# Key norms of the second and third round taken from the diagonals of the keys' products

## The chip, the cores and the metric

One core of one Trainium2 chip runs the whole program. The metric is the device time of one execution in microseconds; lower is better. TensorE is called PE here, VectorE DVE, ScalarE ACT, GpSimd POOL and SyncE, whose queue issues nearly all transfers, SP.

## What is computed

Three stages follow each other. The first is a delta-rule attention over two batches of eight heads, 768 tokens of 48 numbers each; the second an MLP with a rational activation; the third a layer of eight experts with one expert for each token. Cut to what matters:

```
# attention, for each (batch, head):
k_n = k / (np.linalg.norm(k, axis=-1, keepdims=True) + 1e-06)
for t in range(S):
    y[:, :, t] = np.einsum('bhd,bhde->bhe', q[:, :, t], state)
    v_old = np.einsum('bhde,bhd->bhe', state, kt)
    state = state + bt[:, :, :, None] * np.einsum('bhd,bhe->bhde', kt, vt - v_old)
# MLP: 1536 tokens, 384 -> 2048 -> 384
h = x @ w_in
P = a[0] + a[1] * h + a[2] * h2 + a[3] * h3
Q = 1.0 + np.abs(b[0]) * np.abs(h) + np.abs(b[1]) * h2
x = (P / (Q + 1e-06)) @ w_out
# experts: argmax and softmax of x @ w_gate; expert 384 -> 1024 -> 384
h = np.maximum(np.einsum('ecd,edf->ecf', disp, w1), 0.0)
y = np.einsum('ecf,efd->ecd', h, w2)
```

The norm of each key enters twice: in gamma, which is beta divided by the square of (norm + 1e-6), and as nrm, norm + 1e-6, by which the values are multiplied so that the keys need not be divided.

## The kernel before

The 768 tokens are 12 chunks of 64, in three rounds of four chunks. The 16 pairs of batch and head lie in two halves of the partitions, eight pairs in each.

For each round r the following is done. `load_kk(r)` (L138) brings the round's keys to SBUF, with tokens on partitions, in two transfers (L142); they lie in a buffer of the tag "raw", of which there are two, shared with the raw MLP weights that `conv` turns from 64-bit to 32-bit numbers (L188 load, L194 to L207) and later with the raw expert weights (L743). `norm(r)` (L212) squares them on ACT (L216), sums the squares on DVE into ss (L217, two instructions for 32 columns), and works out on 128x32 numbers the root (L222 on DVE, Ln and Exp on ACT, L223 and L224), nrm and gamma (L225 to L231), and gamma's transpose gamT (L233). `gram(n)` (L236) multiplies the keys of chunk n with themselves on PE, and ACT copies 32x32 blocks into Wu. `solve(r)` (L254) inverts the triangular systems of all pairs of the round at once on DVE: a memset of its result buffer on POOL (L258), a transpose in blocks of 32x32 from Wu to bufT (L259), the product with gamma (L262), 31 pairs of a product and a sum (L269, L272), and two transposes at the end (L275, L276).

For each chunk n: `values(n)` (L322) multiplies the values by nrm on POOL (L327, two instructions). `lower(n)` (L280, its products L302 and L304) completes the inverse on PE; `tk` (L335) and `qk` (L345) are products with the keys; U (L365), S (L377) and Y (L389) are the new values, the state and the result, each copied by ACT or DVE; L404 to L412 turn Y to the layout in which the MLP takes it.

The MLP works in 48 tiles of 128x512 numbers, in six blocks of 256 tokens. Each tile has a product h on PE (L460), nine element-wise instructions shared by ACT (L465, L466, L476, L477, and L487 for gh), DVE (L469, L470, L478, L479, L480) and POOL (L467, L468, and L488 for gl), and a product with the second weights on PE (L502, or L520 for the last block). gh and gl are the upper and lower part of the activation. After each block follows the gate of its tokens (L540 to L598). Expert weights come in by L743, are split by ACT (L744) and DVE (L745). The first rows of experts 0 to 2 are computed early, between the last tiles: hidden layer (L808, L812, L813), result y (L825), its weighting yo (L829) and a scatter of rows to the output on POOL (L831). L753 gathers rows for an expert.

What sets the order: each step is entered with `add(name, time, needs, f)`, where the time comes from a table of numbers, PLAN. The steps are emitted by time, those that they need first. A scheduler with a simulated timeline then decides, for each engine, the order in which the instructions stand in its queue; an engine runs its queue strictly in that order. `behind` puts an instruction after the end of a solve. The lines that order the steps in question are these:

```
add(("kk", 1), 2.0, [], lambda: load_kk(1))
add(("kk", 2), PLAN["norm"][2] - 8, [("norm", 1)], lambda: load_kk(2))
add(("values", n), U[n] + r0["values"], [("loads", n), ("y", n - 2), ("norm", r)], lambda n=n: values(n))
```

Of the kernel before, what the change touches and what calls it, by code (L numbers as in the profile page):

```python
# [7 lines left out]
F32 = mybir.dt.float32  # L8
# [5 lines left out]
ALU = mybir.AluOpType  # L14
# [66 lines left out]
def attention_moe_moe(ctx, tc, kT, qT, k, v, beta, w_io, a, b, w_gate, w1, w2, out, dbg=None):  # L81
    nc = tc.nc
# [39 lines left out]
    bufT = A3[:, 5120:6144]  # L122
# [89 lines left out]
    def norm(r):  # L212
        ss = ch.tile([128, 32], F32, tag="ss", name="ss", bufs=1)
        for i in range(2):
            kk = kks.pop((r, i))
            nc.scalar.activation(kk, kk, AF.Square)  # L216
            nc.vector.tensor_reduce(ss[:, 16 * i:16 * i + 16], kk, AX, ALU.add)  # L217

        s0 = ch.tile([128, 32], F32, tag="s0", name="s0", bufs=1)
        nrm = ch.tile([128, 32], F32, tag="nrm", name="nrm")  # L220
        g = ch.tile([128, 32], F32, tag="gam", name="gam", bufs=1)
        nc.vector.tensor_scalar(s0, ss, 1e-35, None, ALU.max)  # L222
        nc.scalar.activation(s0, s0, AF.Ln)  # L223
        nc.scalar.activation(s0, s0, AF.Exp, scale=0.5)  # L224
        nc.vector.reciprocal(g, s0)  # L225
        nc.vector.tensor_tensor(g, g, ss, ALU.mult)
        nc.vector.tensor_tensor(nrm, g, s0, ALU.add)
        nc.vector.tensor_scalar(nrm, nrm, 0.5, 1e-6, ALU.mult, ALU.add)
        nc.vector.reciprocal(g, nrm)
        nc.vector.tensor_tensor(g, g, g, ALU.mult)  # L230
        nc.vector.tensor_tensor(g, g, bt[:, 4 * r:4 * r + 4].rearrange("p c u -> p (c u)"), ALU.mult)  # L231
        gT = ch.tile([128, 32], F32, tag="gamT", name="gamT", bufs=1)
        nc.vector.transpose(gT, g)  # L233
        nrms[r], gams[r] = nrm, gT

# [18 lines left out]
    def solve(r):  # L254

        gT = gams.pop(r)
        Wu = Wub[r % 2]
        nc.gpsimd.memset(bufB, 0.0)  # L258
        nc.vector.transpose(bufT, Wu.rearrange("p t u -> p (t u)"))  # L259
        Lt = bufT.rearrange("p (s t) -> p s t", s=32)  # L260
        A = bufA.rearrange("p (s t) -> p s t", s=32)
# [593 lines left out]
    def add(name, time, needs, f):  # L855
        todo[name] = (time, needs, f)
# [13 lines left out]
    U = PLAN["u"]  # L870
# [17 lines left out]
    for p in range(4, NCH, 2):  # L888
        add(("kT", p), U[p - 7] + r0["kT"] if p > 6 else 1.0, [("qk", p - 8), ("qk", p - 7), ("gram", p - 8), ("gram", p - 7)], lambda p=p: load_kT(p))
    add(("kk", 1), 2.0, [], lambda: load_kk(1))  # L890
    add(("kk", 2), PLAN["norm"][2] - 8, [("norm", 1)], lambda: load_kk(2))
    gens = {r: solve(r) for r in range(3)}
    for r in range(3):
        add(("norm", r), PLAN["norm"][r], [("kk", r), ("solve", r - 1, 8)] + [("values", 4 * r - 5 + c) for c in range(-3, 1)], lambda r=r: behind(norm, r, 0 if r else -1))
        s0, ds = PLAN["solve"][r]
        for i in range(9):
            needs = [("solve", r, i - 1)] if i else [("gram", 4 * r + c) for c in range(4)] + [("norm", r), ("solve", r - 1, 8)]
            if i == 8:
# [3 lines left out]
    for n in range(NCH):  # L902
# [4 lines left out]
        add(("loads", n), U[n - 2] + r0["loads"] if n > 1 else n, [("y", n - 2), ("s", n - 2), ("tk", n - 2)], lambda n=n: loads(n))  # L907
        add(("values", n), U[n] + r0["values"], [("loads", n), ("y", n - 2), ("norm", r)], lambda n=n: values(n))
        add(("qk", n), U[n] + r0["qk"] if n > 1 else PLAN["qk"][n], [("loads", n), ("kT", n - n % 2), ("y", n - 2), ("solve", 0, 8)], lambda n=n: behind(lambda i: qk(i, h_tile if n < 2 else m_tile), n, 0))
# [183 lines left out]
```

## Time and profile before

| | |
|---|---|
| median of 3 runs | 600.73 us (597.03 to 602.11) |
| the profiled execution's own time | 600.51 us |
| its span from the first to the last instruction | 598.7 us |
| PE busy | 502.5 us (84%) |
| DVE busy | 471.3 us (79%) |
| ACT busy | 375.4 us (63%) |
| POOL busy | 289.1 us (48%) |
| bytes moved by DMA | 59.33 MB, mean 99 GB/s |

A share of the whole span is a mean over three stages with different limits; the windows and timelines of the stretches in question tell which engine decides in each. In the rows of a timeline the first number is the start, the second the time from the first instruction's start to the last one's end, both in us; behind them stand engine, line, operation, result<-operands by the program's names, the shapes and how many instructions the row joins. In brackets stands the engine's idle time ahead of the row, and what ended it.

### The profile page before, as it was taken

The page shows a single profiled execution, that of the slowest core. Times are in us where ns is not written, and L with a number is a line of the kernel's source. Part 1 is how long each engine was busy: PE and PEld are TensorE (multiplying, and loading weights), DVE is VectorE, ACT ScalarE, POOL GpSimd, SP SyncE. Part 2 cuts the span into 40 slices and gives each one's busy share as a digit, 9 for nine tenths or more (in the row PEclk, how much of TensorE's full clock was granted, in tenths as well). Part 3 has the DMA queues.
Part 4 walks back from the last instruction along what each step waited for, and adds up shares of the span by engine and source line. Part 5 has one row for each costly group of instructions (what it writes and reads, how often), then busy time and mean ns, then how long its engine had stood idle before and what let it go on. Part 6 is the DMA issues. An engine that isn't in the chain of part 4 may idle for free.

```text
span 598.7 us, 14884 instructions
## 1 busy us (share of the span) xinstructions
PE 502.5 (84%) x6024; PEld 421.4 (70%) x6024; DVE 471.3 (79%) x870; ACT 375.4 (63%) x772; POOL 289.1 (48%) x290
## 2 busy tenths in 40 slices
PE   5515766797898998998999999888999899799993
PEld 5415654576687887777888888677988587677761
DVE  3999998998998999999567648999795688863220
ACT  5632465695799775676797989967774366651110
POOL 8402213966965757653566656469642423021111
PEclk9999866897989989997999999899999999999997
DMA  8901404754451010010010103551043788840000
GB/s 240 281 12 54 121 15 131 176 146 165 140 166 36 1 41 28 2 22 21 27 28 29 28 2 106 160 175 39 1 150 115 227 281 283 282 134 31 18 18 31
DMA packets 42159, 59.33 MB, mean 99 GB/s; under 512 B 25550, under 2 KB 29172, under 8 KB 42082
## 3 DMA queue, kind: packets, MB, share of 16 engines
q1 hardware_dynamic: 40034, 52.78, 29.7%
q0 software_dynamic: 2048, 5.52, 2.8%
q8 instruction: 49, 0.80, 0.6%
q14 instruction: 28, 0.23, 0.1%
HBM read 52.76 MB, written 6.30 MB: 99 GB/s over the span
## 4 chain that ended last, share of the span: by engine, by line
DVE 40%; PE 33%; DMA 8%; issue 8%; ACT 7%; POOL 4%; SPq 0%; DVEq 0%; POOLq 0%; ACTq 0%
PE y L825 7%; DVE A L272 7%; PE h L460 7%; DVE A L269 7%; PE acct L502 6%; DMA ws<-in_w_dram 5%; PE hp L788 4%; DVE ew L745 4%; DVE h L479 2%; DVE pf L469 2%; DVE t L195 2%; DVE pf L480 2%; DVE pf L470 2%; DVE pf L478 2%; POOL gl L488 1%
## 5 line engine op out<-in xcount | busy, mean ns | idle before, releaser
L460 PE MATMUL h<-x,wi 128*128 128x256 f16 x864 | 115.2, 285 | 11.4 <-ACT x L411 5.1
L460 PEld LDWEIGHTS <-wi 128*128 128x128 f16 x864 | 82.3, 102 | 30.9 <-issue 11.1
L488 POOL TENSOR_TENSOR gl<-pf,gh 128x512 fp32r<-128x512 f32 x48 | 67.1, 1399 | 40.5 <-ACT gh L487 34.9
L745 DVE SCALAR_TENSOR_TENSOR ew<-ws,ew 128x768 f16<-128x768 f32 x64 | 67.4, 1073 | 11.1 <-ACT ew L744 9.4
L467 POOL TENSOR_SCALAR zf<-za,cf 128x512 f32<-128x512 f32 x48 | 45.1, 939 | 61.7 <-ACT za L465 61.2
L744 ACT ACTIVATE ew<-ws 128x768 f16<-128x768 f32 x64 | 52.2, 843 | 23.0 <-DMA ws<-in_w_dram 22.3
L468 POOL TENSOR_TENSOR zf<-zf,za 128x512 f32<-128x512 f32 x48 | 64.9, 1352 | 3.3
L788 PE MATMUL hp<-dx,ew 128*128 128x256 f16 (+1 forms) x576 | 53.6, 252 | 6.1 <-DVE hl L794 4.4
L788 PEld LDWEIGHTS <-ew 128*128 128x128 f16 x576 | 47.8, 98 | 11.5 <-issue 6.8
L831 POOL DMA_INDIRECT out_dram<-yo,idx x16 | 16.9, 1056 | 79.5 <-DVE yo L829 70.8
L469 DVE TENSOR_TENSOR pf<-pf,h 128x512 f32<-128x512 f32 x48 | 32.5, 677 | 25.5 <-ACT pf L466 23.0
L825 PE MATMUL y<-ew,hh 128*128 128x384 f16 x208 | 51.7, 326 | 0.0
L269 DVE TENSOR_TENSOR A<-A,A 128x31 f32<-128x31 f32 (+15 forms) x93 | 43.5, 468 | 2.5
L272 DVE TENSOR_TENSOR A<-A,A 128x31 f32<-128x31 f32 (+15 forms) x93 | 43.2, 465 | 2.4
L502 PE MATMUL acct<-wo_h,gl 128*128 128x384 f32 x160 | 41.1, 368 | 4.1 <-POOL gl L488 4.1
L502 PE MATMUL acct<-wo_h,gh 128*128 128x384 f32 x160 | 40.3, 367 | 2.3 <-ACT gh L487 2.3
L478 DVE SCALAR_TENSOR_TENSOR pf<-pf,cf,h 128x512 f32<-128x512 f32 x48 | 35.4, 737 | 6.4 <-ACT h L477 6.2
L476 ACT ACTIVATE za<-zf,qc 128x512 f32<-128x512 f32 x48 | 34.4, 717 | 8.3 <-POOL zf L468 8.1
L502 PE MATMUL acct<-wo_l,gh 128*128 128x384 f32 x160 | 38.4, 354 | 0.0
L466 ACT ACTIVATE pf<-h,cf 128x512 f32<-128x512 f32 x48 | 37.2, 774 | 0.7 <-POOL gl L488 0.6
L793 ACT ACTIVATE hh<-hp 128x512 f16<-128x512 f32 (+1 forms) x32 | 16.0, 507 | 34.3 <-PE hp L788 34.3
L477 ACT ACTIVATE h<-za 128x512 f32<-128x512 f32 x48 | 28.6, 596 | 12.3 <-DVE pf L470 8.4
(188 smaller groups left out, 1226.0 us busy)
## 6 DMA issues: line engine op xcount, KB each, us to landing
ws<-in_w_dram SPq DMA_DIRECT2D x64, 384.0 KB
raw<-in_w_io_dram SPq DMA_DIRECT2D x16, 768.0 KB
rows<-xr SPq DMA_DIRECT2D x12, 192.5 KB
kk<-in_k_dram SPq DMA_DIRECT2D x6, 384.0 KB
A<-in_k_dram SPq DMA_DIRECT2D x24, 96.0 KB
v<-in_v_dram SPq DMA_DIRECT2D x12, 192.0 KB
A<-in_qT_dram SPq DMA_DIRECT2D x24, 96.0 KB
A<-in_kT_dram SPq DMA_DIRECT2D x10, 192.0 KB
```

The source lines that it names most:

```text
L269: nc.vector.tensor_tensor(tmp, A[:, j, n:32].unsqueeze(2).to_broadcast([128, m, n]), T[:, j:n, 0:n].to_broadcast([128, m, n]), ALU.mult)
L272: nc.vector.tensor_tensor(T[:, n:32, 0:n], T[:, n:32, 0:n], tmp, ALU.add)
L460: s1_last[i] = nc.tensor.matmul(h[:, w * m:w * m + w], ww[:, kt, js], x[:, kt, 0:w], start=(n == 0), stop=(n == 8))
L467: nc.gpsimd.tensor_scalar(zf, za, cf[:, 5:6], cf[:, 4:5], ALU.mult, ALU.add)
L468: nc.gpsimd.tensor_tensor(zf, zf, za, ALU.mult)
L478: nc.vector.scalar_tensor_tensor(pf, pf, cf[:, 0:1], h, ALU.add, ALU.mult)
L488: nc.gpsimd.tensor_tensor(gl, pf, gh.bitcast(F32), ALU.subtract)
L502: ends["s2"] = nc.tensor.matmul(acc[blk][t], g[:, o:o + 128], ww[:, j, :], start=(j == 0 and m == 0), stop=(j == 15 and m == 2))
L744: nc.scalar.activation(ws[:, 2 * m, cs], s, AF.Copy, scale=MS)
L745: nc.vector.scalar_tensor_tensor(ws[:, 2 * m + 1, cs], s, MS, ws[:, 2 * m, cs], ALU.mult, ALU.subtract)
L788: nc.tensor.matmul(hp[:, g, 0:ns], w[:, kt, 128 * (f + g):128 * (f + g) + 128], xx[:, kt, 0:ns], start=(n == 0), stop=(n == 8))
L825: nc.tensor.matmul(y, hx[f // 4][:, f % 4, cs], w[:, f, :], start=(n == 0), stop=(n == 23))
```

## The change

In the second and third round (r = 1 and 2) the keys are no longer loaded with tokens on partitions, nor squared and summed. The diagonal of each 32x32 block of the keys' products holds the same sums of squares. `solve(r)` reads them from the transposed blocks, as every 33rd number of a row of bufT, and works out root, nrm and gamma itself. As the blocks are transposed, gamma comes out in the layout that the solve takes, and it is nrm that is transposed back (L281 of the new numbering); beta is transposed for these rounds by `beta_turned` (L249). `values` waits for the solve's first part in place of `norm`. The first round keeps `load_kk` and `norm`. The numbers of PLAN are unchanged. From `root` on the lines of the new kernel are 5 to 25 higher than those of before.

```diff
+        s0 = root(ss)
+        g, nrm = gamma(ss, s0, bt[:, 4 * r:4 * r + 4].rearrange("p c u -> p (c u)"), "gam")
+        gT = ch.tile([128, 32], F32, tag="gamT", name="gamT", bufs=1)
+        nc.vector.transpose(gT, g)
+        nrms[r], gams[r] = nrm, gT
+
+    def root(ss):
 
         s0 = ch.tile([128, 32], F32, tag="s0", name="s0", bufs=1)
-        nrm = ch.tile([128, 32], F32, tag="nrm", name="nrm")
-        g = ch.tile([128, 32], F32, tag="gam", name="gam", bufs=1)
         nc.vector.tensor_scalar(s0, ss, 1e-35, None, ALU.max)
         nc.scalar.activation(s0, s0, AF.Ln)
         nc.scalar.activation(s0, s0, AF.Exp, scale=0.5)
+        return s0
+
+    def gamma(ss, s0, beta_, tag):
+
+        nrm = ch.tile([128, 32], F32, tag="nrm" if tag == "gam" else "ss", name="nrm", bufs=2 if tag == "gam" else 1)
+        g = ch.tile([128, 32], F32, tag=tag, name="gam", bufs=1)
         nc.vector.reciprocal(g, s0)
         nc.vector.tensor_tensor(g, g, ss, ALU.mult)
         nc.vector.tensor_tensor(nrm, g, s0, ALU.add)
         nc.vector.tensor_scalar(nrm, nrm, 0.5, 1e-6, ALU.mult, ALU.add)
         nc.vector.reciprocal(g, nrm)
         nc.vector.tensor_tensor(g, g, g, ALU.mult)
-        nc.vector.tensor_tensor(g, g, bt[:, 4 * r:4 * r + 4].rearrange("p c u -> p (c u)"), ALU.mult)
-        gT = ch.tile([128, 32], F32, tag="gamT", name="gamT", bufs=1)
-        nc.vector.transpose(gT, g)
-        nrms[r], gams[r] = nrm, gT
+        nc.vector.tensor_tensor(g, g, beta_, ALU.mult)
+        return g, nrm
+
+    btT = {}
+
+    def beta_turned(r):
+        btT[r] = const.tile([128, 32], F32, name="btT")
+        nc.vector.transpose(btT[r], bt[:, 4 * r:4 * r + 4].rearrange("p c u -> p (c u)"))
...
-        gT = gams.pop(r)
         Wu = Wub[r % 2]
         nc.gpsimd.memset(bufB, 0.0)
         nc.vector.transpose(bufT, Wu.rearrange("p t u -> p (t u)"))
+        if r:
+
+            ss = bufT[:, 0:1024:33]
+            s0 = root(ss)
+            yield
+            gT, nt = gamma(ss, s0, btT[r], "gamT")
+            nrms[r] = ch.tile([128, 32], F32, tag="nrm", name="nrm")
+            nc.vector.transpose(nrms[r], nt)
+        else:
+            gT = gams.pop(r)
...
-    add(("kk", 1), 2.0, [], lambda: load_kk(1))
-    add(("kk", 2), PLAN["norm"][2] - 8, [("norm", 1)], lambda: load_kk(2))
...
-        add(("norm", r), PLAN["norm"][r], [("kk", r), ("solve", r - 1, 8)] + [("values", 4 * r - 5 + c) for c in range(-3, 1)], lambda r=r: behind(norm, r, 0 if r else -1))
+        if r:
+            add(("beta", r), 1.0, [], lambda r=r: beta_turned(r))
+        else:
+            add(("norm", r), PLAN["norm"][r], [], lambda r=r: norm(r))
...
-            needs = [("solve", r, i - 1)] if i else [("gram", 4 * r + c) for c in range(4)] + [("norm", r), ("solve", r - 1, 8)]
+            needs = [("solve", r, i - 1)] if i else [("gram", 4 * r + c) for c in range(4)] + [("norm", r), ("beta", r), ("solve", r - 1, 8)] + [("values", 4 * r - 5 + c) for c in range(-3, 1)]
...
-        add(("values", n), U[n] + r0["values"], [("loads", n), ("y", n - 2), ("norm", r)], lambda n=n: values(n))
+        add(("values", n), U[n] + r0["values"], [("loads", n), ("y", n - 2), ("norm", r), ("solve", r, 1)], lambda n=n: values(n))
```

DVE's queue in the second round keeps its order; the two reductions ahead of the transpose are gone. The first place shown is DVE's queue around the start of the third solve, A_87 and A_85 being the solve's buffers bufT and bufA or bufB, x_... the MLP's input and pf and h a tile's numbers. Before:

```order
L412 SCALAR_TENSOR_TENSOR x_1879<-xp,x_1878 128x3x64
L470 SCALAR_TENSOR_TENSOR pf<-pf,cf,h 128x512
L480 SCALAR_TENSOR_TENSOR pf<-h,pf 128x512
L259 STREAM_TRANSPOSE A_87<-A_87 128x1024
L412 SCALAR_TENSOR_TENSOR x_1879<-xp,x_1878 128x3x64
L262 SCALAR_TENSOR_TENSOR A_87<-A_87,gamT 128x1024
L269 TENSOR_TENSOR A_87<-A_87,A_85 128x31
```

After; the transpose L273 (L259 before) stands 16 rows ahead of the first row here, and L286 is L262 of before:

```order
L238 TENSOR_TENSOR nrm<-gam,s_2703 128x32
L239 TENSOR_SCALAR nrm<-nrm 128x32
L240 RECIPROCAL gam<-nrm 128x32
L281 STREAM_TRANSPOSE nrm<-nrm 128x32
L502 SCALAR_TENSOR_TENSOR pf<-pf,cf,h 128x512
L503 SCALAR_TENSOR_TENSOR h<-zf,qc,h 128x512
L241 TENSOR_TENSOR gam<-gam 128x32
L504 SCALAR_TENSOR_TENSOR pf<-h,pf 128x512
L242 TENSOR_TENSOR gam<-gam,btT 128x32
L286 SCALAR_TENSOR_TENSOR A_87<-A_87,gam 128x1024
L288 COPY A_85<-gam 128x32
L293 TENSOR_TENSOR A_87<-A_87,A_85 128x31
```

What moved: the chain from ss to gamma, with stages of tiles and parts of a gate between its steps, now stands between the transpose and the product with gamma, where one instruction stood.

The second place is POOL's queue at the end of the second round, with the values of chunk 3 (L327, L351 in the new numbering), the memset of the third solve's buffer (L258, L272) and the mask of the products qk (L352, L376). Before:

```order
L327 TENSOR_TENSOR A_86<-v,nrm 64x8x48 x2
L352 AFFINE_SELECT A_85<-A_85 64x8x64 x2
L327 TENSOR_TENSOR A_86<-v,nrm 64x8x48 x2
L258 MEMSET A_85 128x1024
L207 TENSOR_TENSOR wo_l<-t_851,wo_h 128x384
```

After:

```order
L351 TENSOR_TENSOR A_86<-v,nrm 64x8x48 x2
L376 AFFINE_SELECT A_85<-A_85 64x8x64 x2
L272 MEMSET A_85 128x1024
L351 TENSOR_TENSOR A_86<-v,nrm 64x8x48 x2
L207 TENSOR_TENSOR wo_l<-t_847,wo_h 128x384
```

What moved: the memset, from behind the second of these two multiplications to ahead of it.

The third place is POOL's queue at the end of the MLP, with the gather for an early expert (L753, L777 in the new numbering), gl of the last tiles (L488, L512) and the scatter of the early expert's rows (L831, L855). Before:

```order
L467 TENSOR_SCALAR zf<-za,cf 128x512
L753 DMA ax<-rows,idx_131 128x385
L468 TENSOR_TENSOR zf<-zf,za 128x512
L488 TENSOR_TENSOR gl<-pf,gh 128x512 x2
L831 DMA out_dram<-yo,idx_131 1536x384
L633 TENSOR_TENSOR v_5765<-oh,tid 128x16
```

After:

```order
L491 TENSOR_SCALAR zf<-za,cf 128x512
L777 DMA ax<-rows,idx_131 128x385
L492 TENSOR_TENSOR zf<-zf,za 128x512
L512 TENSOR_TENSOR gl<-pf,gh 128x512 x2
L855 DMA out_dram<-yo,idx_131 1536x384
L512 TENSOR_TENSOR gl<-pf,gh 128x512
L657 TENSOR_TENSOR v_5753<-oh,tid 128x16
```

What moved: the last tile's gl, from ahead of the scatter to behind it.

## Rows read from the trace of the kernel before

**Rows 1.** The page's chain that ended last, its shares by engine.

```profile
DVE 40%; PE 33%; DMA 8%; issue 8%; ACT 7%; POOL 4%; SPq 0%; DVEq 0%; POOLq 0%; ACTq 0%
```

**Rows 2.** Windows: length, then PE, PEld, DVE, ACT, POOL busy us; TensorE clock, DMA.

```profile
54.00:95.00 41.00, 27.37 (x602) 24.58 (x597) 38.55 (x87) 19.31 (x51) 9.14 (x14) 0.77 0.29 79
95.00:166.00 71.00, 57.98 (x785) 46.69 (x785) 66.61 (x83) 52.91 (x118) 53.37 (x42) 0.81 0.52 154
166.00:193.00 27.00, 26.19 (x357) 21.84 (x355) 24.22 (x41) 25.32 (x63) 14.84 (x14) 0.95 0.38 112
193.00:279.00 86.00, 75.92 (x836) 65.27 (x836) 85.18 (x160) 57.96 (x118) 51.57 (x49) 0.97 0.08 20
```

**Rows 3.** Instructions on the tile kk: ns min/median/max, first and last start, shapes.

```profile
L216 ACT ACTIVATE kk<-kk x6: 827/842/843, 7.3 to 170.5; 128x768 f32<-128x768 f32 x6
L217 DVE TENSOR_REDUCE ss<-kk x6: 936/945/952, 8.2 to 173.1; 128x16 f32<-128x768 f32 x6
```

**Rows 4.** Timeline of DVE at the start of the second solve.

```profile
54.52 1.81 DVE L217 TENSOR_REDUCE ss<-kk 128x16 f32<-128x768 f32 x2
```

**Rows 5.** Instructions on the tile gam, one for each round.

```profile
L230 DVE TENSOR_TENSOR gam<-gam x3: 191/191/1257, 15.9 to 181.8; 128x32 f32<-128x32 f32 x3
...
L233 DVE STREAM_TRANSPOSE gamT<-gam x3: 197/211/211, 19.2 to 183.9; 128x32 f32<-128x32 f32 x3
```

**Rows 6.** Instructions of line L264, one for each round.

```profile
L264 DVE COPY A<-gamT x3: 185/188/190, 20.9 to 185.3; 128x32 f32<-128x32 f32 x3
```

**Rows 7.** The page's groups: count, busy us, mean ns, idle time before and its end.

```profile
L460 PE MATMUL h<-x,wi 128*128 128x256 f16 x864 | 115.2, 285 | 11.4 <-ACT x L411 5.1
...
L478 DVE SCALAR_TENSOR_TENSOR pf<-pf,cf,h 128x512 f32<-128x512 f32 x48 | 35.4, 737 | 6.4 <-ACT h L477 6.2
```

**Rows 8.** Windows, DVE's instructions on the tile gam alone, second and third round.

```profile
52.00:64.00 12.00, 1.68 (x7) 0.95 0.42 138
172.00:186.00 14.00, 3.94 (x7) 1.00 0.47 140
```

**Rows 9.** Timeline of DVE at the start of the third solve.

```profile
191.65 1.25 DVE L259 STREAM_TRANSPOSE A<-A 128x1024 f32<-128x1024 f32 x1 [0.97 <-ACT A L250]
...
193.30 1.22 DVE L262 SCALAR_TENSOR_TENSOR A<-A,gamT 128x1024 f32<-128x1024 f32 x1
```

**Rows 10.** Timelines of POOL, PE and ACT at the end of the second solve.

```profile
89.13 1.82 POOL L327 TENSOR_TENSOR A<-v,nrm 64x384 f32<-64x384 f32 x2 [2.24 <-PE S L377]
95.84 1.30 POOL L258 MEMSET A<- 128x1024 f32 x1 [4.90 <-DVE t L194]
...
90.40 0.67 PE L365 MATMUL U<-A,A 112*64 112x48 f32 x16
...
96.94 0.58 PE L460 MATMUL h<-x,wi 128*128 128x256 f16 x2 [5.13 <-ACT x L411]
...
97.23 0.30 ACT L366 ACTIVATE A<-U 64x192 f32<-64x192 f32 x1
```

**Rows 11.** Timelines of POOL, PE and ACT at the end of the MLP.

```profile
450.77 2.77 POOL L488 TENSOR_TENSOR gl<-pf,gh 128x512 fp32r<-128x512 f32 x1 [8.10 <-ACT gh L487]
453.71 1.04 POOL L831 DMA_INDIRECT out_dram<-yo,idx  x1 [0.16 <-issue]
...
448.21 4.06 PE L825 MATMUL y<-ew,ax 128*128 128x384 f16 x24 [0.95 <-DVE ax L813]
...
453.60 0.38 PE L520 MATMUL acc<-gl,wo_h 128*128 128x256 f32 x1 [1.09 <-POOL gl L488]
...
446.58 0.84 ACT L744 ACTIVATE ew<-ws 128x768 f16<-128x768 f32 x1 [1.62 <-DMA ws<-in_w_dram]
...
448.17 0.84 ACT L744 ACTIVATE ew<-ws 128x768 f16<-128x768 f32 x1
...
450.08 0.61 ACT L487 ACTIVATE gh<-pf 128x512 fp32r<-128x512 f32 x1
```

**Rows 12.** Instructions of line L488, all 48 tiles.

```profile
L488 POOL TENSOR_TENSOR gl<-pf,gh x48: 1259/1284/2775, 120.5 to 450.8; 128x512 fp32r<-128x512 f32 x48
```

## The prediction

> **What bounds the kernel now.** I read the chain that ended last, then the windows over the stretches that the change touches, then the timelines around both solves and around the last MLP tile. The chain is spread over DVE (40%) and PE (33%) [rows 1], so no engine's total decides; each stretch is asked for itself. In the windows [rows 2] the reader compares an engine's busy time with the length of the stretch. From 54 to 95 us, where the second solve runs, DVE works 38.55 of 41.00 us and PE only 27.37: DVE decides. From 95 to 166 DVE is still first, with 66.61 of 71. From 166 to 193 PE works 26.19 of 27.00 and DVE 24.22: PE decides, DVE has 2.8 us to spare. From 193 to 279, where the third solve runs, DVE works 85.18 of 86. Work taken from DVE is thus worth its length in the two solve stretches, and little between 166 and 193.
>
> **What goes, and the second round.** In the second and the third round two loads of keys go, two squares on ACT and two reductions on DVE. One reduction lasts 936 to 952 ns, one square 827 to 843 [rows 3]: 1.88 us of DVE and 1.7 us of ACT a round. The second round's two reductions stand at 54.52 for 1.81 us, with no idle time around them [rows 4], in the stretch that DVE decides, and the order of everything behind them on DVE is kept. Added are a transpose of the norm and one of beta, and gamma's own transpose goes: one more 128x32 transpose, 0.21 us [rows 5]. So the second solve's first product and all behind it come 1.81 - 0.21 = 1.6 us earlier, if nothing takes it back. The small chain of the norm stood behind the solve's transpose already; its two waits for ACT stay covered by the same weight conversions.
>
> The sum of squares is now every 33rd number of a row, and no row shows such a read. The nearest is the copy L264, which writes 128x32 at that stride in 185 to 190 ns [rows 6], like a dense step. I price the stride at nothing; bounds 0 and 0.2 us a round.
>
> Of the loads I count nothing: SP's later transfers go out earlier, but the conversions that use them stand in DVE's kept order. ACT's 1.7 us in the third round lie in a stretch where it works 25.32 of 27 us and PE more [rows 2]: bounds 0 and 1.7 us gained, I take 0, the row in which another engine has less idle time.
>
> **The third round.** Its reductions and its chain lay between 172 and 186 us, where DVE has slack. There the seven steps of gamma took 3.94 us, against 1.68 in the second round [rows 8]. Now the chain comes after the third solve's transpose (191.65 [rows 9]), in or at the edge of the stretch that DVE fills. The order shows the solve's first product not two instructions behind the transpose but 26, with stages of three tiles between. At the end of the third solve DVE has done one more tile's stages than before, about four at 737 ns [rows 7] and two short ones, 3.4 us, and that work is then missing behind it. So DVE's total decides. If tile stages that came later fill the slack before 193, the round is 1.9 us shorter; if they don't, what went was slack and nothing is gained. I take the middle, **-0.9**, with bounds -1.9 and 0.
>
> How long the moved chain lasts depends on GpSimd. L230 takes 191 ns twice and 1257 once [rows 5]. The chain has four such steps with two inputs. Unhindered it costs 1.68, so 2.3 less than counted; with each of the four at 1.26 it costs 1.68 + 4 x 1.07 = 6.0, 2.0 more. I keep 3.94 and carry -2.3 and +2.0 into the range.
>
> The reductions never left 936 to 952 ns, while L230 spread up to 1257 [rows 3, 5]. The Trainium skill, SBUF — State Buffer, section "Who interferes with whom", says that a DVE instruction with two inputs in SBUF contends with a GpSimd instruction that reads SBUF, and that a reduction on this chip never contends. The two rows agree. By this rule the change removes what is immune and moves what is not into the fullest stretch, and the third round would end up to 2.0 us later, not 0.9 earlier.
>
> **The wait that GpSimd's new order adds.** The values of chunk 3 used to be multiplied at 89.13, ahead of the memset at 95.84 [rows 10], which needs the second solve's last transposes. Now they stand behind it. Queued behind the values: U of chunk 3 on PE (90.40), ACT's copies of U (97.23), the first MLP tiles (96.94) [rows 10]. With the solve 1.6 us earlier the memset starts at 94.24; then 1.30 for it, 1.82 for the values and 0.67 for U give 98.0, so the copies come 0.8 us later than before. PE has two matmuls of the first tile ahead of this and the rest, which ran from 96.94, behind the state updates: up to 1.8 us later. The second round is worth -1.6 if that is off the path, +1.8 if it is on it; I take the middle, **+0.1**.
>
> **The tail of the MLP.** On GpSimd the last tile's product gl now stands behind the scatter of the early expert's rows. Before, that expert's y began at 448.21, and gl (450.77, 2.77 us) released the last tile's matmuls at 453.60 [rows 11], 5.39 us after y's begin. Now: the scatter starts 5.50 after y's begin (453.71) and takes 1.04, then gl takes 1.28 as usual (the median of its 48 [rows 12]) to 2.77: the matmuls restart 7.8 to 9.3 us after y's begin, 2.4 to 3.9 later. PE's new order has 16 matmuls more of the tile before to fill with, 2 us, and y may start earlier for lack of them in front. So 0 to about +3.7; I take **+1.9**. Behind it come the last gate, the lists and the gather for the experts, one after the other, and nothing covers them.
>
> **Sum**, from the profiled execution's own 600.51 us (span 598.70 and 1.81 around it; 0.2 below the median of 600.73): +0.1 - 0.9 + 1.9 gives **601.6 us**.
>
> **The rivals.** *A, nothing to measure*: the sum; its own range is 598 to 604, where each term keeps to its inner half. *B, faster*: the relief is passed on in full and the tail is filled. -1.6 and -1.9 give 597.0; with the chain unhindered, -2.3, 594.7; with ACT's 1.7 us, 593.0. For it: DVE fills both solve stretches. Against it: the third round's work lay in the slack. *C, slower*, by the last tile's start alone: ACT's order now has three more weight conversions L744 ahead of the last tile's za copy L477. In the old times the third of them ran from 448.17 for 0.84 [rows 11], to 449.01. From there two copies on ACT, L477 and gh, at gh's 0.61 [rows 11], and between them five instructions on DVE, three stages and two conversions, at 0.74 at least [rows 7]: gh ends at 453.9 at the earliest, against 450.69, 3.2 us later, and gl after it. Where weights land late, a conversion adds a wait like the 1.62 us that one had there [rows 11]: three of them make it 8.1. So 603.7 to 608.6, centre 606.2. It decides above 4 us, where PE's 16 matmuls and an earlier y are used up, and is over 1% from 6.2 us on. For it: the order, and a stretch where nothing waits in reserve. Against it: weights that landed early let ACT run them through. *D, late norm*: the values of chunks 8 to 11 now wait for the third solve, and their steps on PE stand one tile of L460 further back, 115.2/48 = 2.4 us [rows 7]. If the last tiles wait for them: 602.9. Against it: PE has other tiles to do.
>
> **How the numbers follow.** A 0.36, B 0.25, C 0.32, D 0.07. The likeliest is A: 601.6. A measurement of this kernel can tell about 1% from no change, so the bounds are 594.7 and 606.7. Just under half of B lies below: faster 0.12. Just under half of C lies above: slower 0.15. The rest, 0.73, is within 1%. The range 594.5 to 608.5 leaves out B's lower part (0.11) and C's upper end (0.03), and some for what I have not seen.
>
> **What would show it.** Right: no reductions at 54 us and the memset near 94.2; the values of chunk 3 after it and U's copies near 98; the third solve's first product later than 193.30; in the tail the scatter ahead of the last gl, and the last tile's matmuls up to 3.7 us later, set against y's begin. Wrong: the first tile before 96 us (the swap harmless); steps of the third chain mostly above 1 us; the last tile earlier against the experts' gather than it was; a difference that grows between 279 and 440 us, where I expect none.

## The result and the profile after

Over 18 runs each, the changed kernel takes 604.09 us (600.45 to 607.18) against 600.55 us (597.03 to 605.6): a ratio of 1.0054, with a 95% interval of 1.0034 to 1.0074. By the ratio that is 3.2 us slower, small but clear of the noise. The forecast was 601.6 us, 1.1 us slower, so the time lies in the range; the sections below show that the sum came near it by luck: both of its main terms were far too small, and the errors cancelled.

The profiled execution of the changed kernel took 600.45 us, its fastest run, 3.6 us below its median; the one of before took 600.51, close to its median. So the two profiles are level, and what the change costs on average shows only in part. A second profile of the same kernel, taken at 605.69 us, is used below where it matters.

The first view is the windows of the changed kernel, with the columns of [rows 2]:

```profile
54.00:95.00 41.00, 25.35 (x550) 22.56 (x546) 38.32 (x89) 19.57 (x52) 9.82 (x14) 0.67 0.22 55
95.00:166.00 71.00, 58.22 (x836) 48.60 (x836) 67.86 (x82) 52.36 (x118) 52.87 (x42) 0.84 0.55 166
166.00:193.00 27.00, 26.28 (x381) 22.46 (x376) 18.81 (x31) 26.10 (x65) 18.82 (x18) 1.00 0.22 58
193.00:279.00 86.00, 78.54 (x894) 67.16 (x894) 82.53 (x178) 60.35 (x122) 49.44 (x47) 0.98 0.08 20
```

Against [rows 2], DVE is relieved by 5.4 us between 166 and 193, and between 193 and 279 PE does 58 instructions more and DVE 18 more, DVE in 2.65 us less busy time. So the middle did get faster. In this profile the last tile's first ACT copy (za) starts at 427.81, against 436.05 before: 8.2 us ahead, where the sum had foreseen 0.8. Yet the last tile's final matmuls end at 455.96, against 455.77. All of it went in the last 28 us of the MLP. The timelines of DVE, POOL and PE of the changed kernel there, the lines that answer to [rows 11]:

```profile
433.47 0.67 DVE L493 TENSOR_TENSOR pf<-pf,h 128x512 f32<-128x512 f32 x1
439.05 0.15 DVE L795 COPY gg<-ax 128x1 f32<-128x1 f32 x1 [4.90 <-DMA ax<-rows,idx]
439.12 0.74 DVE L502 SCALAR_TENSOR_TENSOR pf<-pf,cf,h 128x512 f32<-128x512 f32 x1
...
432.90 1.53 POOL L777 DMA_INDIRECT ax<-rows,idx  x1 [0.16 <-issue]
...
451.39 1.04 POOL L855 DMA_INDIRECT out_dram<-yo,idx  x1 [6.16 <-DVE yo L853]
452.46 1.27 POOL L512 TENSOR_TENSOR gl<-pf,gh 128x512 fp32r<-128x512 f32 x1
...
443.30 4.32 PE L849 MATMUL y<-ew,ax 128*128 128x384 f16 x13 [3.61 <-DVE ax L837]
447.84 2.61 PE L849 MATMUL y<-ew,ax 128*128 128x384 f16 x11
453.79 0.38 PE L544 MATMUL acc<-gl,wo_h 128*128 128x256 f32 x1 [1.19 <-POOL gl L512]
```

DVE stands still for 4.90 us in a copy of 128 numbers (L795, the gate values of early expert 2), until the gather that POOL issued at 432.90 has landed. Behind it in DVE's queue are the stages of the last two tiles and the split of the early expert's hidden layer (L837), for which PE waits 3.61 us. Before the change the same copy had no wait:

```profile
444.29 0.14 DVE L771 COPY gg<-ax 128x1 f32<-128x1 f32 x1
```

It stood behind more work there, and the gather had landed. In the five traces in which the copy waits, the gather is there 4.2 to 5.3 us after its end on POOL (434.43 to 439.05 here); why it takes that long was not tested. The scatter ahead of gl, on which the prediction put the tail's cost, is there as well, but comes after this.

### The profile page after: what moved, and what is told of

The parts are those of the page before. It is cut to its first block, busy times and chain, and to the rows that moved or that the text cites. A ratio compares the mean times of both kernels' runs of the same rounds, so it can differ in the third digit from the quotient of the medians.

```text
span 598.6 us, 14872 instructions
## 1 busy us (share of the span) xinstructions
PE 496.7 (83%) x6024; PEld 418.0 (70%) x6024; DVE 454.5 (76%) x868; ACT 373.9 (62%) x768; POOL 293.4 (49%) x290
## 4 chain that ended last, share of the span: by engine, by line
PE 34%; DVE 32%; ACT 9%; DMA 8%; issue 8%; POOL 6%; SPq 0%; DVEq 0%; ACTq 0%; POOLq 0%
PE acct L526 8%; PE h L484 7%; PE y L849 7%; DVE A L293 6%; DVE A L296 6%; PE hp L812 4%; DMA ws<-in_w_dram 4%; DMA raw<-in_w_io_dram 2%; DVE h L503 2%; POOL gl L512 2%; POOL zf L491 2%; DVE pf L502 2%; DVE t L195 2%; ACT ew L768 2%; DVE t L194 2%
## 5 line engine op out<-in xcount | busy, mean ns | idle before, releaser
L484 PE MATMUL h<-x,wi 128*128 128x256 f16 x864 | 110.6, 278 | 11.6 <-ACT x L435 5.4
L484 PEld LDWEIGHTS <-wi 128*128 128x128 f16 x864 | 81.0, 100 | 28.8 <-issue 13.0
L512 POOL TENSOR_TENSOR gl<-pf,gh 128x512 fp32r<-128x512 f32 x48 | 68.1, 1422 | 40.1 <-ACT gh L511 31.4
L491 POOL TENSOR_SCALAR zf<-za,cf 128x512 f32<-128x512 f32 x48 | 47.0, 981 | 49.4 <-ACT za L489 48.9
L769 DVE SCALAR_TENSOR_TENSOR ew<-ws,ew 128x768 f16<-128x768 f32 x64 | 62.3, 993 | 9.1 <-ACT ew L768 8.9
L768 ACT ACTIVATE ew<-ws 128x768 f16<-128x768 f32 x64 | 52.4, 840 | 18.8 <-DMA ws<-in_w_dram 18.1
L855 POOL DMA_INDIRECT out_dram<-yo,idx x16 | 17.2, 1073 | 85.2 <-DVE yo L853 76.6
L502 DVE SCALAR_TENSOR_TENSOR pf<-pf,cf,h 128x512 f32<-128x512 f32 x48 | 35.5, 740 | 15.3 <-ACT h L501 15.1
L493 DVE TENSOR_TENSOR pf<-pf,h 128x512 f32<-128x512 f32 x48 | 32.6, 679 | 17.7 <-ACT pf L490 17.7
L293 DVE TENSOR_TENSOR A<-A,A 128x31 f32<-128x31 f32 (+15 forms) x93 | 40.2, 432 | 2.6
L526 PE MATMUL acct<-wo_h,gl 128*128 128x384 f32 x160 | 39.8, 362 | 1.9 <-POOL gl L512 1.9
L296 DVE TENSOR_TENSOR A<-A,A 128x31 f32<-128x31 f32 (+15 forms) x93 | 37.2, 399 | 2.5
L511 ACT ACTIVATE gh<-pf 128x512 fp32r<-128x512 f32 x48 | 29.9, 627 | 13.4 <-DVE pf L504 12.6
L817 ACT ACTIVATE hh<-hp 128x512 f16<-128x512 f32 (+1 forms) x32 | 16.1, 507 | 35.2 <-PE hp L812 35.1
```

The lines of the kernel that those rows point to most:

```text
L293: nc.vector.tensor_tensor(tmp, A[:, j, n:32].unsqueeze(2).to_broadcast([128, m, n]), T[:, j:n, 0:n].to_broadcast([128, m, n]), ALU.mult)
L296: nc.vector.tensor_tensor(T[:, n:32, 0:n], T[:, n:32, 0:n], tmp, ALU.add)
L484: s1_last[i] = nc.tensor.matmul(h[:, w * m:w * m + w], ww[:, kt, js], x[:, kt, 0:w], start=(n == 0), stop=(n == 8))
L491: nc.gpsimd.tensor_scalar(zf, za, cf[:, 5:6], cf[:, 4:5], ALU.mult, ALU.add)
L502: nc.vector.scalar_tensor_tensor(pf, pf, cf[:, 0:1], h, ALU.add, ALU.mult)
L512: nc.gpsimd.tensor_tensor(gl, pf, gh.bitcast(F32), ALU.subtract)
```

## The experiments

All ratios are to the kernel before, run beside it on the same chip, with 95% intervals; its medians there were 601.21, 603.56, 602.36 and 602.4 us. The first four runs asked what the tail costs and what the prediction's two swaps on POOL cost.

**The changed kernel again.** No edit.

> The changed kernel once more, unedited, for a second profile. In its first profile (600.45 us, 3.6 below its median) the last tile's za copy stood 8.2 us earlier than before (427.81 against 436.05) and the last tile's final matmuls not (455.96 against 455.77). Theory 1, the tail eats what the middle gains: about 603 to 605, and again a last tile that starts 5 to 9 us earlier and ends level or later. Rival, the first profile was a lucky middle: a last tile that starts no earlier than before.

Measured: 604.39 us, ratio 1.0043 (1.0015 to 1.007). In its profile (605.69 us) the last tile's za copy is at 431.86, 4.2 us ahead of before, and its final matmuls end at 460.72, 4.9 us behind. So in this execution, 1.3 us above its median, the middle gains about 4 us and the tail loses about 9. The first profile had the same tail and a quicker middle.

**The gate copy behind the last tile's DVE stages.**

```diff
-        ex[e] = expert_x(gather(e, 0, 1, idx0, [ax[0][:, o:o + ROW]]), m_tile, to)
+        xds = gather(e, 0, 1, idx0, [ax[0][:, o:o + ROW]])
+        if e == 2:
+            with tc.issue_after(ends["pf"].ins):
+                ex[e] = expert_x(xds, m_tile, to)
+        else:
+            ex[e] = expert_x(xds, m_tile, to)
```

> The changed kernel, where DVE's copy of the gate values of the third early gather is put behind the last tile's last DVE stage; with that the scheduler also puts the last tile's gl ahead of the scatter. In the profile of the change DVE stood 4.90 us in this copy, waiting for the gather, with two tiles' stages queued behind. Theory 1 (the copy is the wait): the last tile's final matmuls end 4 to 5 us earlier, 599 to 600.5 us. Theory 2 (the scatter ahead of gl is the wait, as predicted): about 1.2 us earlier, 602 to 603.5. Theory 3 (weights or gathers set the end of the tail): no change, 604.

Here `ends["pf"]` is the last tile's last DVE stage. With this edit the order also has the last tile's gl ahead of the scatter, so the next run takes the scatter alone. Measured: 596.01 us, ratio 0.9924 (0.9895 to 0.9953). That is 8.4 us less than the change beside it, and faster than the kernel before. The timelines of DVE, POOL and PE in its tail:

```profile
433.91 0.67 DVE L493 TENSOR_TENSOR pf<-pf,h 128x512 f32<-128x512 f32 x1
434.51 0.73 DVE L502 SCALAR_TENSOR_TENSOR pf<-pf,cf,h 128x512 f32<-128x512 f32 x1
...
445.35 0.15 DVE L795 COPY gg<-ax 128x1 f32<-128x1 f32 x1
...
445.77 1.28 POOL L512 TENSOR_TENSOR gl<-pf,gh 128x512 fp32r<-128x512 f32 x1 [2.45 <-ACT gh L511]
447.20 1.04 POOL L855 DMA_INDIRECT out_dram<-yo,idx  x1 [0.15 <-issue]
...
439.91 2.28 PE L849 MATMUL y<-ew,ax 128*128 128x384 f16 x13
442.26 1.96 PE L849 MATMUL y<-ew,ax 128*128 128x384 f16 x11
447.10 0.38 PE L544 MATMUL acc<-gl,wo_h 128*128 128x256 f32 x1 [0.73 <-POOL gl L512]
```

The stage L502 follows L493 at once, where it was 5.65 us behind (433.47 to 439.12). y begins 3.4 us earlier and also runs faster: its 13 and 11 matmuls span 2.28 and 1.96 us in place of 4.32 and 2.61. Theory 1 holds, and its price was too low. From the last tile's za copy to the end of its gl the tail is 7.1 us shorter than in the change's first profile and 7.8 than in the second (table below). Theory 1 counted the copy's wait alone; on top came y's slower run at a lower clock (last section) and the scatter that waited for y.

**Only the scatter behind the last tile's gl.** `early_y` is issued behind the last gl in the same way; the gate copy stays.

> The changed kernel, where only the scatter of the early expert's rows is put behind the last tile's gl on GpSimd; DVE's copy stays where it is. In the profile of the change gl started at 452.46 behind the scatter, its gh was there at 450.02, and PE was busy with the tile before until 452.6. Theory 1: the last matmuls restart at 452.6 in place of 453.79, 1.2 us, so 602.5 to 603.5 us, and the 4.90 us wait for the gather is still there. Theory 2 (the scatter is the cost): 2.4 to 3.7 us, 600.5 to 601.7.

Measured: 603.41 us, ratio 1.003 (1.0002 to 1.0059), 1.0 us under the change beside it; the two intervals overlap. The gate copy still waits, 5.12 us in its profile. The prediction's mechanism alone is worth about a microsecond, if anything; the rest goes with the gather's wait.

**The memset back behind the values of chunk 3.** `solve(2)`'s memset is issued behind `values(3)`.

> The changed kernel, where the memset for the third solve is put back behind the values of chunk 3 on GpSimd, as before the change; nothing else moves. By the prediction the swap costs between 0 and 3.4 us in the second round, so 600.7 to 604. If the first tiles are not on the path there: 604, with the first gl earlier than the 129.12 us of the change and the later tiles unmoved.

Measured: 601.22 us, ratio 0.9995 (0.997 to 1.002), 3.2 us under the change, at the upper end of what the prediction had for the swap. Its profile (600.29 us) doesn't show where: the last tile starts at 427.89, as in the change's first profile (427.81). Two later runs, the next one and the second round's part with the same edit, ask whether this is a cost of its own.

**Both single edits together.**

> Both single edits on the changed kernel: the memset behind the values of chunk 3, and the gate copy behind the last tile's DVE stages. Alone they gave -3.2 us (601.2) and -8.4 us (596.0) against the change's 604.4. If they are separate costs: 592 to 594. If the memset's 3.2 us are only an effect of where the clock falls, or are taken up before the tail: 595 to 597.

Measured: 594.09 us beside 603.56, ratio 0.9846 (0.9804 to 0.9889): 1.5% faster than before, the best of all. By the ratios it is 0.8% under the gather edit alone, which ran beside other runs of the kernel before; the two intervals nearly touch.

**Control: the gather edit on the kernel before.**

> Control: the same edit of the gate copy on the kernel before. There the copy (444.29) waited for nothing, and its tail was 19.7 us from the last tile's start to its final matmuls against 28 of the change. Theory 1 (the copy costs only where it waits for the gather): no change, within 1 us of before. Rival (the edit makes any tail shorter): 594 to 598.

The control carries the scatter edit too, which changes nothing in that order: gl is ahead of the scatter there already. Measured: 602.54 us, ratio 0.9991 (0.9959 to 1.0024). The edit does nothing where the copy does not wait. The tail's loss belongs to the order that came with the change.

**The second round's part alone.** The condition in `solve` and in the steps is `r == 1`; the third round keeps `load_kk(2)` and `norm(2)`.

> The change in the second round alone; the third round loads and sums its keys as before. The scheduler's order has the memset ahead of the values of chunk 3, as in the full change, and in the tail the gate copy behind four weight conversions and gl ahead of the scatter. Theory 1: -1.6 us for the reductions and +3.2 for the swap, nothing in the tail: 1 to 2 us above before, 602 to 603. Rival (the cost of the change sits in the third round or its tail alone): 598.5 to 599.5.

Measured: 597.45 us, ratio 0.9905 (0.9874 to 0.9936), by the ratio 5.7 us faster, against both expectations and with the swap in place.

**The third round's part alone.** The same with `r == 2`.

> The change in the third round alone. The order has the values of chunk 3 ahead of the memset, as before, and in the tail the same rows as the full change, the gate copy ahead of two tiles' stages and gl behind the scatter. Theory 1: the tail costs 8 to 9 us and the middle gives back what it gave in the full change without the swap and the second round, some 5 us: 602.5 to 604.5, with a last tile that starts about 5 us earlier than before. Rival (the tail's loss needs the middle's early start, so both vanish): 600 to 601.

Measured: 615.88 us, ratio 1.0226 (1.0187 to 1.0264), 12 us above the kernel before beside it by the medians, 14 by the ratio, and far beyond both expectations. Its gate copy, in the timeline of DVE:

```profile
449.35 0.15 DVE L795 COPY gg<-ax 128x1 f32<-128x1 f32 x1 [5.50 <-DMA ax<-rows,idx]
```

The tail has the known loss (26.3 us in the table below, 17.5 before). In the middle the last chunk's x is copied at 397.25 us against 386.48 before, but the last tile starts only 1.5 us late in this profile, which is of its fastest run, 2.9 us under the median.

**The third round's part alone, with the gather edit.**

> The change in the third round alone, with the gate copy behind the last tile's DVE stages. Alone the third round stood at +2.3% (615.9 against 603.6), with 5.50 us of DVE idle before the gate copy in the tail. If the tail's cost is the same 8 us as in the full change: 1.0% above before, and the rest, some 5 us, is what the third round costs in the middle without the second. If the middle alone makes it late: 1.8% or more.

Measured: 608.63 us beside 602.36, ratio 1.0099 (1.0068 to 1.0129). The edit gives 1.3%, close to the 1.2% that it gave on the full change (1.0043 to 0.9924): the tail's loss is the same term in both. The remaining 6 us are the middle: in this profile, 2.7 us above its median, the last tile starts at 444.50, 8.5 us late.

**The second round's part alone, with the memset behind the values.**

> The change in the second round alone, with the memset behind the values of chunk 3. If the swap costs here what it cost in the full change (3.2 us): 1.5% below before, level with the two single edits on the full change. If the swap's 3.2 us came from the third round's later start: 1.0% below before, as without it.

Measured: 596.64 us, ratio 0.9898 (0.9863 to 0.9933), the same as without the edit. So the swap shows no price of its own here; 3.2 us (0.5%) lie at the edge of what the two intervals allow. In the full change its 3.2 us came with the rest of that order.

The parts do not add: second round -5.7 us, third round +6 with its tail mended, both with the tail mended -4.6. What they have in common is the third solve. In its 31 products and 31 sums DVE spent, by the windows (before, then the change, then the second round alone; the first of each pair of rows is the products, the second the sums):

```profile
193.00:279.00 86.00, 20.19 (x31) 0.97 0.08 20
193.00:279.00 86.00, 20.28 (x31) 0.97 0.08 20
```

```profile
203.00:277.00 74.00, 17.92 (x31) 0.98 0.09 23
203.00:277.00 74.00, 14.28 (x31) 0.98 0.09 23
```

```profile
199.00:278.00 79.00, 16.93 (x31) 0.96 0.09 21
199.00:278.00 79.00, 16.58 (x31) 0.96 0.09 21
```

40.5 us before, 32.2 with the change, 33.5 with its second part alone, for the same 62 instructions; the third part alone has 35.2. The first round's 62 take 22.4 us, while POOL works 3.42 us between 24 and 53. This is far more than the reductions that went (1.8 us a round). By the timelines about as many of the 62 steps overlap an instruction of POOL in each of the four kernels (39, 36, 38 and 40), but 27 of them are over 0.3 us longer than the shortest of the same step in the kernel's three rounds before, 18 with the change, 20 and 22 in its second and third part alone; each of these overlaps one. Two runs tested whether POOL makes the difference.

**The kernel before with a late third solve.** Nothing is removed; only the product with gamma is put behind tile 11's last DVE stage.

```diff
+        if r == 2:
+            with tc.issue_after(ends["pf", 11].ins):
+                nc.vector.scalar_tensor_tensor(A, Lt, -1.0, gT.unsqueeze(1).to_broadcast([128, 32, 32]), ALU.mult, ALU.mult)
```

> The kernel before with all its loads, squares and reductions; only the third solve's product with gamma is put behind the last DVE stage of tile 11, where the change has it (3 tiles of stages later than before). Its tail has the gate copy behind four weight conversions and gl ahead of the scatter. Theory 4: the change's gain in the middle is not the removed work but the third solve's new place among the tiles: its 62 products and sums took 40.5 us on DVE before and 32 to 33.5 with the change (22.4 with GpSimd idle, in the first round), since fewer of them meet a GpSimd instruction. Then here 31 to 35 us, and 594 to 598 against a before of 601 to 603. Theory 1 as it was (the removed reductions give the gain): 40 us in the solve, no change or 1 us slower for the late start.

Measured: 603.82 us, ratio 1.0033 (1.0 to 1.0066). The steps took 36.6 us, 4 less than before, but their first began at 213.3 in place of 194.5, later than the change has it (206.3), and the solve ended at 287.6, 9 us later. Four us less in the steps gave no gain here. Theory 4 falls in that form.

**The kernel before with POOL out of tiles 8 to 22.**

```diff
+        if 8 <= i <= 22:
+            nc.scalar.activation(zf, za, AF.Identity, bias=cf[:, 4:5], scale=cf[:, 5:6])
+        else:
...
+        if 8 <= i <= 22:
+            nc.scalar.activation(gl, pf, AF.Copy)
```

> The kernel before, with all its loads, squares and reductions, where GpSimd takes no part in the MLP stages of tiles 8 to 22: their zf and gl come from one ACT copy each, without the square of the activation and without the lower part (both are left out, so the MLP's result is another), and the gate copy in the tail stands behind the last tile's DVE stages. Theory 5: the third solve's 62 steps took 40.5 us before and 22.4 in the first round because they wait out GpSimd's instructions, and the change's gain in the middle is that it has 8 us less of this. Then here 23 to 26 us in these steps, the third solve ends 8 to 15 us earlier, and the last tile starts 4 to 10 us earlier. Rival (the steps are slow for another reason, their strides or PE's reads): 38 to 41 us in them.

In these tiles the kernel leaves out the square in zf and the lower part of the activation, and its gate copy of the tail stands behind the last tile's stages. Measured: 596.95 us beside 602.4, ratio 0.9907 (0.9879 to 0.9935). The two windows again:

```profile
198.00:261.00 63.00, 11.87 (x31) 1.00 0.07 17
198.00:261.00 63.00, 10.93 (x31) 1.00 0.07 17
```

22.8 us: without POOL's tile stages beside them, the steps are as short as in the first round, and the solve ended 18 us earlier (260.3). Theory 5 holds for the steps. The last tile's za copy came 4.4 us earlier, so of 17.7 us on DVE a quarter reached it. In this kernel ACT does the stages in POOL's place: between 193 and 279 it works 82.16 of 86 us, PE 82.20 and DVE only 75.03, so DVE no longer decides there.

The tail in numbers from the traces, from the last tile's za copy to the end of its gl:

| kernel | za starts | gl ends | between, us |
|---|---|---|---|
| before | 436.05 | 453.55 | 17.5 |
| the change | 427.81 | 453.73 | 25.9 |
| the change again | 431.86 | 458.49 | 26.6 |
| third round alone | 437.51 | 463.80 | 26.3 |
| the change, scatter edit | 433.83 | 457.63 | 23.8 |
| the change, gather edit | 428.25 | 447.05 | 18.8 |
| both single edits | 426.64 | 445.50 | 18.9 |
| second round alone | 431.75 | 448.52 | 16.8 |

## Why the prediction came out as it did

**The relief of the second round.** Confirmed for what it named, and too small: no reductions at 54 us, the transpose at 54.37 in place of 56.24, 1.9 us earlier, without the two reductions of [rows 4] ahead of it, and the memset at 92.35 where the prediction had 94.2. The steps of the second solve were held up less too (22.9 us in place of 23.9), so it ended 3.1 us earlier (92.23 against 95.35) where the term was 1.6. The part alone gave 5.7. Where the rest of that arose is not shown. In that kernel the third solve's steps fell from 40.5 to 33.5 us, as fewer of them were held up by POOL; but they fell to 35.2 in the third round's part alone and to 36.6 with the late solve as well, and neither of those was faster.

**The swap on POOL.** As foreseen the values of chunk 3 came behind the memset. The timelines of POOL and ACT of the change, for [rows 10]:

```profile
92.35 1.22 POOL L272 MEMSET A<- 128x1024 f32 x1 [5.72 <-DVE A L300]
93.64 2.51 POOL L351 TENSOR_TENSOR A<-v,nrm 64x384 f32<-64x384 f32 x2
...
96.94 0.32 ACT L390 ACTIVATE A<-U 64x192 f32<-64x192 f32 x1
```

U's copy came at 96.94, against 97.23 before and 98.0 in the sum. But this U is not chunk 3's, as the prediction had it: ACT makes two such copies (L366) a chunk, and these are the sixth, chunk 2's, which read nothing of chunk 3's values. Chunk 3's own first copy is at 118.13, 2.5 us later than before (115.64); the third round's part alone, with the old order on POOL, has it at 119.06. PE's first two matmuls of the first tile came at 94.65, before the 96 us that the prediction had named as the sign of a harmless swap, and that tile's za copy was level (102.64 against 102.80). The first gl ended 7.3 us later (129.12 against 121.82), but four tiles on the delay was gone (tile 4's za 6.7 us earlier). The range of 3.4 us held, 3.2 us came out in the full change and nothing in the second round alone. To give the swap one price was wrong; what around it makes the 3.2 us is not shown.

**The third round.** The forecast was -0.9, bounds -1.9 and 0. The moved chain itself cost less than counted, 1.9 us for its six steps on gamma and the norm's transpose, where 3.94 were kept. The timeline of DVE of the change has these of its steps, the lines for [rows 5] and [rows 9]:

```profile
192.31 1.25 DVE L273 STREAM_TRANSPOSE A<-A 128x1024 f32<-128x1024 f32 x1 [0.20 <-ACT A L265]
...
199.76 0.50 DVE L237 TENSOR_TENSOR gam<-gam,A 128x32 f32<-128x32 f32 x1
200.29 0.19 DVE L238 TENSOR_TENSOR nrm<-gam,s 128x32 f32<-128x32 f32 x1
...
203.62 0.18 DVE L242 TENSOR_TENSOR gam<-gam,btT 128x32 f32<-128x32 f32 x1
203.84 1.23 DVE L286 SCALAR_TENSOR_TENSOR A<-A,gam 128x1024 f32<-128x1024 f32 x1
204.98 1.26 DVE L288 COPY A<-gam 128x32 f32<-128x32 f32 x1
```

Only one of its two-input steps was held up, for 0.3 us; the read at every 33rd number (L237) took 0.50 here and 0.21 in the second round, so the stride costs at most 0.02 against the 0.19 of a dense step. The copy behind the chain (L288) was held up by 1.1 us: 1.26 here, 0.19 in the second round. The solve's first product came 11.7 us later and its end 2.3 us earlier. Rival D did not come about: chunk 8's values were multiplied at 218.29, 1.1 us earlier than before. But to this round the runs give no single price: with its tail mended it adds 6 us alone, and 0.2% (1.1 us, inside the intervals) on top of the second round's part. Between the two cases the third solve ends at 290.5 and 275.8. What in the second part's order spares the third this loss is not settled; a late place of the solve alone does not (603.82 us).

**The rule that was weighed in the wrong place.** The Trainium skill, SBUF — State Buffer, section "Who interferes with whom", says that a DVE instruction with two SBUF inputs contends with a GpSimd instruction that reads SBUF. The prediction applied it to four small steps and put up to 2.0 us on them. In this case's traces it governs the 62 steps of the third solve: 22.8 us without POOL's stages, 40.5 with them. The prediction held the rule against the change alone; with the change these steps are 8.3 us shorter. How much of that reached the end is not shown: of the 17.7 us without POOL's stages a quarter reached the last tile.

**The tail.** This is the step that failed. The prediction read the order on POOL and on ACT, found the scatter ahead of gl and three more weight conversions, and took +1.9 (0 to 3.7). The loss was 8.4 us by the medians and 8 to 9 by the table, and its cause was in the queue that was not read there: DVE's, where the new order puts the gate copy, and so the landing of a gather, ahead of the last two tiles' stages. The two gather edits show it, and the control shows that the edit gains nothing where the copy doesn't wait. In the prediction's own measure, from y's begin to the restart of the last matmuls, it forecast 7.8 to 9.3 us; it was 10.5 (443.30 to 453.79), as y took 7.2 us in place of 4.1. In that profile the scatter kept gl waiting for 2.4 us (gh ended at 450.02, gl started at 452.46), about half of it while PE was still busy with the tile before; put behind gl, it gave about 1 us.

Rival C, a loss by the weight conversions ahead of L501 (L477 before), did not come about. The three conversions ran without a wait, the last until 439.65, and then ACT stood idle for DVE, whose stages the gate copy had delayed. The timeline of ACT of the change:

```profile
441.27 0.60 ACT L501 ACTIVATE h<-za 128x512 f32<-128x512 f32 x1 [1.62 <-DVE pf L494]
```

**The sum.** By the medians of runs side by side the middle gave -5.2 us (596.01, the change with its tail mended, against 601.21) and the tail took +8.4 (to 604.39): +3.2. The prediction had -0.8 and +1.9. Both terms had the right sign and were too small, by factors of six and four. The middle came out near rival B's with an unhindered chain (-5.8), the tail at the upper end of rival C's loss (8.1), by another cause. That the time fell near the forecast, and the difference under 1%, was luck: two larger errors cancelled.

## What to carry to other kernels

Where a scheduler writes the order, taking work out redraws every queue behind it: read the new order of each engine for instructions that wait for a DMA and have other work queued behind them, not only the engine where a swap is noticed first. The removed instructions may be the smaller part: here the same 62 steps on DVE changed by 8 us through what POOL did beside them, though how much of that reached the end stayed open. A loss in the tail like this one can be mended by a single ordering edge; with that edge the change was worth making, and with a second one it was 1.5% faster than before.

## What the runs showed of the hardware

A small DVE step with two inputs that meets POOL's 128x512 products can last until POOL's instruction ends. The timelines of DVE and POOL of the kernel before, at the start of the third solve:

```profile
195.23 1.25 DVE L272 TENSOR_TENSOR A<-A,A 128x31 f32<-128x31 f32 x1
196.51 1.20 DVE L269 TENSOR_TENSOR A<-A,A 128x60 f32<-128x60 f32 x1
197.75 1.20 DVE L272 TENSOR_TENSOR A<-A,A 128x60 f32<-128x60 f32 x1
...
195.12 1.28 POOL L488 TENSOR_TENSOR gl<-pf,gh 128x512 fp32r<-128x512 f32 x1
196.37 1.27 POOL L468 TENSOR_TENSOR zf<-zf,za 128x512 f32<-128x512 f32 x1
197.60 1.27 POOL L488 TENSOR_TENSOR gl<-pf,gh 128x512 fp32r<-128x512 f32 x1
```

Three steps of 31 to 60 numbers, 0.2 us each elsewhere (206.28 0.20 in the change's timeline), go in lockstep with three instructions of POOL, 3.65 us in all. Not every step that meets POOL is held up (27 of the 39 that overlap one here). And a copy with one input can be: L288 in the change, 1.26 us from 204.98, beside POOL's gl that ran from 204.45 for 1.75.

An idle PE cost twice here. The windows of the change and of the gather edit around the early expert's y (columns as in [rows 2]):

```profile
442.00:450.00 8.00, 6.70 (x25) 3.53 (x25) 7.30 (x11) 2.25 (x4) 1.85 (x1) 0.57 0.62 162
```

```profile
439.00:445.00 6.00, 6.00 (x44) 4.47 (x43) 6.00 (x10) 3.25 (x6) 1.37 (x1) 1.00 0.70 178
```

After the 3.61 us wait the granted clock is 0.57, mostly the lower level of 1.2 GHz, and y's 24 matmuls stretch over 7.2 us with the gap between them (443.30 to 450.45); without the wait it is 1.00, 2.4 GHz, and they take 4.3 (439.91 to 444.22). In the five traces in which the gate copy waits (4.5 to 5.6 us), y's first 13 matmuls take 3.8 to 4.3 us; in the three kernels of the change with the copy moved, 2.28. The same shows between two executions of one kernel. The change's first and second profile between 160 and 167 us:

```profile
160.00:167.00 7.00, 6.95 (x127) 5.98 (x123) 6.95 (x9) 6.29 (x14) 6.48 (x5) 1.00 0.36 115
```

```profile
160.00:167.00 7.00, 5.85 (x48) 4.97 (x49) 7.00 (x9) 4.73 (x10) 4.03 (x4) 0.53 0.35 115
```

127 matmuls at the full clock, 48 at 0.53; in the second execution PE had stood idle for 2.30 us until 161.15. It is 2.5 us behind the first from there on (tile 8's za copy at 175.32 against 172.85), with the same program. That is half of the 5.2 us between the two; what makes the rest is not shown.
